# Sparse attention and a gated feed-forward block on one core: first loads, first mask, one pair's transposes and the written-out order are changed

## The chip, the core and the metric

The kernel runs on one core of a Trainium2 chip. The core has five engines with a queue of instructions each: TensorE (PE, matrix products and transposes), VectorE (DVE), ScalarE (ACT, here the exponentials, tanh and part of the copies), GpSimd (POOL, here masks at the start and the issue of the loads that convert fp32 to bf16) and SyncE (SP, which issues transfers and computes nothing). An engine takes its queue in order; an instruction that waits for a semaphore holds up everything behind it on that engine. The metric is the device time of the core in microseconds (us): the median of three runs. One more execution is recorded by the hardware profiler, and the profile, the trace and all durations come from that one.

## The reference

Inputs are q, k and v of 4 batches x 8 heads x 768 positions x 64, a table of three sampled blocks for each of 24 blocks of 32 positions, and the weights of the second half, in fp32.

```python
scores = scale * np.matmul(q, k.transpose(0, 1, 3, 2))
mask = np.abs(blk_i - blk_j) <= window
mask = mask | (blk_i == 0) | (blk_j == 0) | (blk_i == n_blocks - 1) | (blk_j == n_blocks - 1)
for qb in range(n_blocks):
    for kb in sampled_blocks[qb]:
        mask[qb * block:(qb + 1) * block, kb * block:(kb + 1) * block] = True
scores = np.where(mask, scores, -1000000000.0)
...
x = softmax(scores) @ v          # heads side by side: 4 x 768 x 512
h = np.maximum(x @ w_in, 0.0)    # 512 -> 1024
conv_out[s] = sum(conv_w[k] * h[s + k - 1] for k in range(3))
out = (h * sigmoid(conv_out)) @ w_out   # 1024 -> 512
```

## The kernel before

**Work and tiles.** Two heads of a batch make a pair; there are 16 pairs P0 to P15, four to a batch. Half a batch (384 query positions) is a segment; segment n has 18 units, the last half batch is split into a segment of 256 and one of 128 positions (12 and 6 units), 144 units in all. A unit is eight blocks of 128 x 128 scores: products on PE into a psum tile `st` (line 745, two operations `s`, six products in most units), one exponential of 128 x 1024 on ACT into `pt` (line 756, `exp`), and products with the values into `av` (line 778, two operations `av` of four products, the value tile carrying a column of ones for the sums). When all units of a pair in a segment are through, DVE takes the reciprocal and normalises into `xtok` (lines 695 and 697), and the result is transposed into `xT`: in segments 0, 7 and 8 on PE (line 716), in 1 to 6 by a transposing transfer that SP issues (line 706, called the x transfers here, four to a segment). Then come the products with w_in (line 886, `f1`, which needs all four transposed pieces of its segment), relu on ACT or DVE (lines 906 and 908), the convolution as three scaled copies and two additions on DVE (938, 946), tanh on ACT (985), the gate on DVE (988, 993), the products with w_out (824, `f2`; the last block 809), and the copy and transfer out (829 to 832).

**Mask.** A masked score gets -8000 added before the scaling, by 24 more rows of contraction: rows 64 to 87 of the query side hold a 24-row table of the allowed blocks, those of the key side the indicator of the block (`nblk`). The table `aadd` is made at the start: POOL writes the band and the last row (`A` and `row23`), DVE the edges (`a3`), and when the sampled blocks have landed, `a4` multiplies three comparisons with them into it (lines 294 to 300). Two groups of products (`w24`, line 314) spread it, and four copies (`m_q0`, `m_q1`, `m_k` twice) put the rows into the first slot tiles `e` and `o`; later slots copy them (`m_h1`, `m_slot`).

**Queries and keys.** Pairs below `NPE` (6 here) are transposed on PE: `kq_transposes` loads k and half of q, then 6 key transposes (line 472) and 4 query transposes (line 509) go through a psum tile, and DVE or ACT copies them into the slot (lines 342 and 346); the second query half is loaded later (`nq`) and takes 4 more transposes. The other pairs go through the crossbar: `kq_crossbar` loads k and q, two transposing transfers on SP (`xb`, line 584, first k, then q) write `stg`, and two copies of 64 x 1536 fill the slot. Pair 0's first loads are fp32 transfers on the hardware queues of SP and ACT (lines 253 to 261), cast by `cast_q` and `cast_k`; all other loads are issued by POOL and convert on the way. Some POOL loads have a small copy ahead of them (`pace`, lines 420 and 659) that holds the queue until an earlier load or an exponential is through.

**The order.** Nothing is scheduled at run time. The program builds a list of operations (1,796 of them, numbered as they are made), and the string ORDER says in which order they are put on the queues: two characters are the number of an operation to base 64, then a letter for the engine where it has a choice (P, A, V, G, S), then the buffer for each tile that it takes. `put_down` reads it. The order of the instructions on each engine is thus the order of the string. Ahead of the first products PE does `NWARM` products on zeros (line 1011).

Of the kernel before, what the change touches and what calls it, by code (L numbers as in the profile page):

```python
# [7 lines left out]
FP32 = mybir.dt.float32  # L8
# [3 lines left out]
ALU = mybir.AluOpType  # L12
# [8 lines left out]
0c00010d02030e0f0g1k01l1w01y10508090a0b06070H0I041z1K11M21N1Y21f01s10G0j0h0K0E0i0l0/V30qA11Arn1rorprqrrrsrtru  # L21
rvrwrxryrzrArBrCrDrErFrGrHrIrJrKrLrMrNrOrPrQrRrS13014A0rTrUrVrWrXrY0n00rA0pA12V19110V1aV0m01611bV15V0oArZr+r/
1c01dV0v0F0x0u17A18A1jV00ws0s1s2s34B04C4G11eA4D04H4L04M4I14N21m14E11p01nV11oV1qA1rV4Q14R4F4S34V04J4K4W4O52153
4P4T4U4X4570581A14Y5455900A0z0y1xV11BV21D05c15d4Z0555h05i561FV1CV1EV5e15j20s15q15r0t5s35a5b5f5g5v05w1O05k5A15B
5x41R15F05G0B4+01LV21PV35C51QV1TV1SV4/1g05l5K15L5H01hV1iV0k1t11vV1ZV31uV0V1+34i1/0W4j0X4k2a04l0Y4m1G04n0Z4o2c0
4p2d4q0+4r2o14s1U14t2q14u2r4v2w24w2y24x2z4y5m15n5M15t15T05u5U5V25y5z5005Y15Z0L15D5E5I610625J5N5O05W5+30C0M5P2
0U5Q661675X5o16346f06g51V06855pV0P5/606465696a6k16l6h06m16b06c0D5R06i16j6d16p06q5SA6u16v6r26w32bA46eVhJ1hK0J
hLV00OhM06z0hN0ThOVi506AhS16B4hT6H16IhUV6J5i6i76nhP06M0hQ6N1H1hRA6O0id1if1JV1IVi8i96o6R16s6ShV0hW6T16W06t6X721
hXA6Y2ia20121V4736xhY06y6ChZ6D06K7706L6P787430Q22Vie6E1igh+Vi216Q7c17d6U6V2306Zi36+7947e525A6Fih6/224Vil2706G1
i4A7h07i7m17517j0iih/11V0761WV1XV7ai07b7f7n7gi1A7o17u07v7k7l2e07w27z17A7p7q02h17B37E07F7J17K7G4imibit3iniu2fV0  # L30
ic0ij2gVioikip7r02jViv2iV7siw7L5iH07R07S7T0iqirixis7x7y7CiI7D7H7W17X7/080iB17IiC7M7N7U17Y1812712s02t7tiy7O17P
iz2pV0iA2xV10S2uV17Q2A12B7V841858907Z7+828aiJiD8638h18i8387888b48j58m08n8o02E04z2G2H32602J2I4AiEiK8c8r18s8w08x
iLA0iFV18e22vV8fiQ1iN0iOiR8t18y2iPAiSVj90jbja8E18F8d08k8J08KiW18liT08G38L48O18P8Q58p8q8u8T08U8V0iUiX2CV22DVjc
2FV2iVVjdiYA8Y18Z8v8z8A940j008H1iZ1j18+1jejh1jijjj2V8B0jk8C2O2k12R2P12S0959622U2T991i+8I8M9a8N2708R29V28Vjli/A
9b39e08S8W9f8X8/900979j19k9g49l5jm911jp2jfjqj61j79r0j8V92jsjr98j309s9c9d9h9w19x9i8g22K02V1938D2W2L9t09y12l1j4
2nV2mVj5Vjgjn9B09C9m9n9u19G19H9v9z9A9D29I39L09M9N5jt9o2jx3jyjoju9pjAjzjBjvjw9q9EjL19T19FjX09U9Y0jY9Z9J9V09+1jC
jM9K9O9P0a119Wa29Xa60a79/a0jNjZa33ae1a809Q1jDjEj+jOj/V2afaj0akk40a4a5k530311jPA3ag2k11k2a9ao1al3k3A12Z2+23332
383903b3c22MV32XV4k6V9R2YVkp02NVkqkrks0Napat0kj0auaq43e3dav5k71k8aaab0ackkk9AklAay1azaG0aHkm1knka0kbah1aiamaI1
aA0koVkcAktkN12QV3kx2kOkykAaL0aMkd1anaraskg0aN2kukzawkv2/V4aQ1aRaxaBaD2aS3aV0khkekiAkfAkF3kBaC0aJaKaOaWb11aX4
jR0b2jS9S0341iGb35kCjTaPb60jUb7aTjF1jVA1b81bb1aUaYbcaZjGkQkGkIkHaEbd2kw1kJkDa+1kEa/kPkRbg0bhbi3kKjHb41b5kV0b9  # L40
bl1bmbajIbt0jQiM353f03gjWaFadb0jJV3bn4kSbebfbjkWbuk/1by136V0kTkLkM3hV1kUbv5l0bkbzbobD03iV37Vbq2bEkXl1bA13j3m
3k13n03r3o3p3qbF0l23aV0l3A0bI1bJkYbQ0bRkZV1l81l9bK2bS3l50l6l7Abr3lV1laVlt0lulvlwlxbV1bWbp0le1bwb+0b/bxbBbX4c05
# [71 lines left out]
def kernel(  # L114
# [24 lines left out]
    SEQ = "nq0 nq1 k4 q4 w0 v4 w1 nq2 w2 k5 q5 w3 v5 nq3 k6 q6 v6 k7 q7 v7 nq4 nq5"  # L139

    CONV_PE = {8: (0, 1, 2, 3)}

    sb = ctx.enter_context(tc.tile_pool(name="sb", bufs=1))
# [903 lines left out]
```

## Time and profile before

| | |
|---|---|
| median of 3 runs | 213.57 us (213.3 to 215.49) |
| profiled execution | 214.17 us |
| its span, first to last instruction | 212.4 us |
| granted TensorE clock, mean | 0.999 |
| busy PE / DVE / ACT / POOL | 199.5 / 183.5 / 192.4 / 61.4 us |
| moved by DMA | 25.21 MB |

The page's second part shows the span in 40 slices of 5.3 us, busy share in tenths:

```profile
PE   8799999989999996999999997999999999999993
...
DVE  5889979999789985999999986999889939999870
ACT  5999999999999986999999996999999999997822
```

And its part on queues says which transfers there are: q0 holds POOL's converting loads, q1 the transfers of SP, q10 those of ACT.

```profile
q0 software_dynamic: 19728, 11.05, 43.4%
q1 hardware_dynamic: 30408, 13.05, 29.2%
q10 hardware_dynamic: 576, 0.69, 0.9%
```

In a row of the timeline stand start, length, engine, line, operation, output and inputs, shapes, count, and in brackets how long the engine stood idle before it and what released it. A busy PE is not PE at its peak, as its products overlap. Waits are inferred from semaphores.

### The profile page before, as it was taken

What the parts mean: (1) busy time and instruction counts of PE and PEld (TensorE: products, weight loads), DVE (VectorE), ACT (ScalarE), POOL (GpSimd) and SP (SyncE); (2) the same over time, 40 slices, a digit from 0 to 9 for tenths busy, and PEclk for the clock granted to TensorE, in tenths of its full rate; (3) what the DMA queues carried; (4) which work ended last, traced back from release to release, by engine and by line L of the source; (5) the groups of instructions that cost most, each with busy time, mean ns of one, the idle gap of its engine ahead of it and who ended that gap; (6) DMA issues with size and microseconds to landing.
All of it is one profiled execution on the core that took longest, in us unless ns stands there. A gap on an engine that the chain in (4) does not pass through costs nothing.

```text
span 212.4 us, 6868 instructions
## 1 busy us (share of the span) xinstructions
PE 199.5 (94%) x2708; PEld 155.6 (73%) x2727; DVE 183.5 (86%) x579; ACT 192.4 (91%) x253; POOL 61.4 (29%) x117
## 2 busy tenths in 40 slices
PE   8799999989999996999999997999999999999993
PEld 7689978877778774777688775777687877775752
DVE  5889979999789985999999986999889939999870
ACT  5999999999999986999999996999999999997822
POOL 8937456530732522300716363600000000000000
PEclk9999999999999999999999999999999999999999
DMA  6999999996899499894679999990231132020205
GB/s 169 184 197 200 165 115 116 124 146 95 112 141 119 90 138 117 154 202 106 90 99 173 124 133 210 209 176 20 65 93 22 22 128 91 0 84 28 94 0 198
DMA packets 50743, 25.21 MB, mean 119 GB/s; under 512 B 36800, under 2 KB 47768, under 8 KB 50712
## 3 DMA queue, kind: packets, MB, share of 16 engines
q0 software_dynamic: 19728, 11.05, 43.4%
q1 hardware_dynamic: 30408, 13.05, 29.2%
q10 hardware_dynamic: 576, 0.69, 0.9%
q8 instruction: 21, 0.34, 0.7%
q14 instruction: 10, 0.08, 0.1%
HBM read 23.08 MB, written 6.29 MB: 138 GB/s over the span
## 4 chain that ended last, share of the span: by engine, by line
PE 50%; DVE 20%; ACT 16%; DMA 9%; issue 4%; SPq 1%; ACTq 0%; DVEq 0%
PE st L745 15%; PE mix L824 11%; ACT pt L756 11%; PE mix L886 10%; PE av L778 8%; DMA xT<-xtok 6%; DVE m L938 5%; DVE m L946 3%; DMA stg<-nat 2%; DVE gT L993 2%; DVE hE L908 2%; DVE o L346 2%; PE st L1011 2%; ACT hE L906 1%; DVE e L346 1%
## 5 line engine op out<-in xcount | busy, mean ns | idle before, releaser
L756 ACT ACTIVATE pt<-st 128x1024 bf16<-128x1024 f32 x144 | 140.9, 1037 | 4.0 <-PE st L745 3.1
L778 PE MATMUL av<-vt,pt 128*128 128x65 bf16 x1152 | 61.8, 193 | 0.0
L778 PEld LDWEIGHTS <-pt 128*128 128x128 bf16 x1152 | 53.2, 97 | 11.4 <-issue 2.0
L886 PE MATMUL mix<-xT,winb 128*128 128x384 bf16 (+2 forms) x288 | 54.4, 307 | 4.0 <-DMA xT<-xtok 3.0
L938 DVE TENSOR_SCALAR m<-hE,cw 128x382 bf16<-128x382 bf16 (+2 forms) x192 | 50.1, 317 | 2.1 <-ACT hE L906 1.8
L745 PE MATMUL st<-o 88*128 88x128 bf16 (+1 forms) x240 | 44.8, 229 | 0.3 <-ACT pt L756 0.3
L824 PE MATMUL mix<-woutb,gT 128*128 128x512 bf16 x157 | 43.6, 379 | 1.3 <-DVE gT L993 0.3
L745 PE MATMUL st<-o,e 88*128 88x128 bf16 (+1 forms) x228 | 44.0, 233 | 0.3 <-ACT pt L756 0.2
L745 PE MATMUL st<-e,o 88*128 88x128 bf16 (+1 forms) x224 | 42.4, 234 | 1.2 <-ACT pt L756 1.2
L745 PE MATMUL st<-e 88*128 88x128 bf16 (+1 forms) x208 | 41.5, 239 | 0.5 <-ACT pt L756 0.2
L745 PEld LDWEIGHTS <-o 88*128 88x128 bf16 x464 | 34.7, 97 | 8.6 <-issue 1.7
L745 PEld LDWEIGHTS <-e 88*128 88x128 bf16 x436 | 33.8, 97 | 9.3 <-issue 0.9
L946 DVE TENSOR_TENSOR m<-m 128x764 bf16<-128x764 bf16 (+2 forms) x64 | 33.5, 532 | 0.3
L886 PEld LDWEIGHTS <-winb 128*128 128x128 bf16 x288 | 23.6, 97 | 10.0 <-issue 3.5
L985 ACT ACTIVATE m<-m 128x764 bf16<-128x764 bf16 (+2 forms) x32 | 26.4, 832 | 0.6 <-DVE m L946 0.6
L420 POOL COPY pace<-pt 1x1 bf16<-1x1 bf16 x24 | 8.3, 345 | 54.9 <-ACT pt L756 54.9
L824 PEld LDWEIGHTS <-gT 128*128 128x128 bf16 x184 | 15.3, 97 | 10.0 <-DVE gT L993 0.7
L906 ACT ACTIVATE hE<-mix 128x384 bf16<-128x384 f32 (+2 forms) x38 | 18.6, 503 | 3.9 <-PE mix L886 2.7
L908 DVE TENSOR_SCALAR hE<-mix 128x384 bf16<-128x384 f32 x26 | 14.2, 553 | 8.0 <-PE mix L886 7.0
L697 DVE TENSOR_TENSOR xtok<-av,rcp 128x384 bf16<-128x384 f32 (+2 forms) x36 | 18.2, 505 | 0.3
L993 DVE TENSOR_TENSOR gT<-m,hE 128x764 bf16<-128x764 bf16 (+3 forms) x36 | 18.0, 508 | 0.5 <-ACT hE L906 0.3
L240 POOL DMA_DIRECT2D nat<-in_q_dram x23 | 16.8, 733 | 3.3 <-issue 2.7
(93 smaller groups left out, 167.0 us busy)
## 6 DMA issues: line engine op xcount, KB each, us to landing
out_dram<-o2s SPq DMA_DIRECT2D x22, 256.0 KB, 2.1
nat<-in_k_dram POOLq DMA_DIRECT2D x15, 192.0 KB, 5.0
vn<-in_v_dram POOLq DMA_DIRECT2D x15, 192.0 KB, 5.5
nat<-in_q_dram POOLq DMA_DIRECT2D x6, 192.0 KB, 5.3
winb<-in_moe_w_in_dram POOLq DMA_DIRECT2D x2, 512.0 KB, 6.6
woutb<-in_moe_w_out_dram POOLq DMA_DIRECT2D x4, 256.0 KB, 4.9
nat<-in_q_dram POOLq DMA_DIRECT2D x9, 96.0 KB, 4.7
nq<-in_q_dram POOLq DMA_DIRECT2D x6, 96.0 KB, 4.6
```

Of the source, the lines that this page charges most:

```text
L697: nm = op("norm", {"DVE": t_dps(128 * C)}, lambda e: nc.vector.tensor_tensor(out=xtok_t[xk.index][:, 0:C].rearrange("p c h d -> p h c d"), ...
L745: nc.tensor.matmul(out=st[:, 128 * x:128 * (x + n_)], lhsT=QK[kc % 2][s][0:88, 1, hh, kc // 2, :], rhs=QK[par][s][0:88, 0, hh, idx:idx + n ...
L756: nc.scalar.activation(out=pt_t[ptb.index], in_=st_t[stb.index], func=AF.Exp, bias=0.0, scale=0.125)
L778: nc.tensor.matmul(out=o[:, off:off + 65], lhsT=pt_t[ptb.index][:, 128 * x:128 * x + 128], rhs=V_t[vslot_b[P].index][:, hh, kc, 0:65], sta ...
L824: nc.tensor.matmul(out=acc(), lhsT=gT_t[gb.index][:, ffc, 128 * t:128 * t + 128], rhs=woutb[:, ffc, :], start=(ffc == 0), stop=(ffc == NFF ...
L886: nc.tensor.matmul(out=mix_t[hb.index][:, w1 * y:w1 * y + w1], lhsT=winb[:, fc, 128 * ffc:128 * ffc + 128], rhs=xT_t[xt_buf[n].index][:, f ...
L906: nc.scalar.activation(out=dst, in_=src, func=AF.Relu, bias=0.0, scale=0.5)
L908: nc.vector.tensor_scalar(out=dst, in0=src, scalar1=0.5, scalar2=0.0, op0=ALU.mult, op1=ALU.max)
L938: nc.vector.tensor_scalar(out=m_t[cb.index][:, x, y, 0:w], in0=hE_t[heb.index][:, f0 + y, t0 + x:t0 + x + w], scalar1=cw[:, x, f0 + y:f0 + ...
L946: nc.vector.tensor_tensor(out=m[:, a_, :, 0:w], in0=m[:, a_, :, 0:w], in1=m[:, b_, :, 0:w], op=ALU.add)
L985: th = [op("tanh", {"ACT": t_act(2 * w) + 0.04}, lambda e, cb=cb, w=w: nc.scalar.activation(out=m_t[cb.index][:, 0, :, 0:w], in_=m_t[cb.in ...
L993: nc.vector.tensor_tensor(out=gT_t[gtb.index][:, f0:f0 + 2, t0:t1], in0=m_t[cb.index][:, 0, :, 0:w], in1=hE_t[heb.index][:, f0:f0 + 2, 1 + ...
```

## The change

Six things change.

1. **First loads.** The keys of head 1 (`k1`) move from ACT's queue to SP's, behind the sampled blocks; ACT issues only the first query load.
2. **First mask.** The table holds 1 for masked and 0 for allowed; -8000 is put into the key rows instead (`k_rows`). `a4` is one comparison of all three sampled blocks with the column index (24 x 3 x 24, integers) and one minimum over those three and `A`, in place of a cast and three multiplications; the cast of the column index (`col`, line 287) goes.
3. **One shorter transpose.** The second query transpose of pair 0, head 0 takes 64 columns instead of 128, so it no longer reads columns that belong to head 1's cast.
4. **Pair 5** goes through the crossbar (`NPE` 5): 6 key and 8 query transposes and their six copies are replaced by two transfers on SP and two staged copies; its second query half comes with the first load.
5. **Warm products**: 60 instead of 45.
6. **ORDER** is new throughout (1,803 operations).

```diff
-    NF, NPE = 4, 6
+    NF, NPE = 4, 5
...
-    NWARM = 45
+    NWARM = 60
...
     q0 = first_q(0, "ACT", -22, [])
-    k1 = first_k(1, "ACT", -21, [q0])
     ld_sb = op("ld_sb", {"SP": 0.46}, lambda e: nc.sync.dma_start(out=sbi, in_=sampled_blocks.bitcast(I32)), -21,
                after=[k0], lat=1.8)
-    q1 = first_q(1, "SP", -20, [ld_sb])
+    k1 = first_k(1, "SP", -20, [ld_sb])
+    q1 = first_q(1, "SP", -20, [k1])
...
     def a_rand(e):
-        nc.vector.tensor_copy(out=rf, in_=sbi[:, 0:6:2])
-        for r in range(3):
-            nc.vector.scalar_tensor_tensor(out=aadd if r == 2 else A, in0=colidx, scalar=rf[:, r:r + 1], in1=A,
-                                           op0=ALU.not_equal, op1=ALU.mult)
+        nc.vector.tensor_tensor(out=hit[:, 0:3], in0=colidx_i.unsqueeze(1).broadcast_to([NB, 3, NB]),
+                                in1=sbi[:, 0:6:2].unsqueeze(2).broadcast_to([NB, 3, NB]), op=ALU.not_equal)
+        nc.vector.tensor_reduce(out=aadd, in_=hit.rearrange("j r c -> j c r"), axis=mybir.AxisListType.X, op=ALU.min)
...
     def k_rows(dst, x):
-        return lambda e: dcopy(e, dst[64:88, 1, 0], nblk.rearrange("j (p c t) -> j t c p", c=3, t=2)[:, x])
+        def fn(e):
+            to, src = dst[64:88, 1, 0], nblk.rearrange("j (p c t) -> j t c p", c=3, t=2)[:, x]
+            if e == "ACT":
+                nc.scalar.activation(out=to, in_=src, func=AF.Copy, bias=0.0, scale=-8000.0)
+            else:
+                nc.vector.tensor_scalar(out=to, in0=src, scalar1=-8000.0, scalar2=None, op0=ALU.mult)
+        return fn
...
-                        nc.tensor.transpose(out=t[:, 128 * pos:128 * pos + 128], in_=src()[:, c0:c0 + 128], identity=ident)
+                        w_ = 64 if P == 0 and g == 0 and hh == 0 and y == 1 else 128
+                        nc.tensor.transpose(out=t[0:w_, 128 * pos:128 * pos + 128], in_=src()[:, c0:c0 + w_],
+                                            identity=ident)
```

ORDER can't be read by eye. Decoded by the numbering of the list, the old and the new string put these on the queues. On which engine operations stand that could stand on two:

| operation | before | after |
|---|---|---|
| copies of the mask rows (`m_k`, `m_q0`, `m_q1`) on ACT / DVE | 4 / 0 | 2 / 2 |
| half query casts of pair 0 on ACT / DVE | 0 / 2 | 1 / 1 |
| query copies on ACT / DVE | 3 / 23 | 6 / 16 |
| key copies on ACT / DVE | 3 / 11 | 3 / 9 |
| staged copies on DVE | 20 | 22 |
| value copies on ACT / DVE | 2 / 14 | 0 / 16 |
| relu on ACT / DVE | 38 / 26 | 37 / 27 |
| output copies on ACT / DVE | 16 / 9 | 18 / 7 |

PE's queue up to the first scores (k0, k1 key transposes of head 0 and 1, q likewise, a number for warm products), and ACT's:

```text
PE  before  32, k0, 6, w24, q0, w24, k1, 3, q1, 4, scores
PE  after   34, k0, 7, q0, w24, w24, 7, k1, 9, q1, 3, scores
ACT before  m_k, cast_k, k_cp, m_k, m_q1, m_q0, k_cp, k_cp, q_cp, exp, exp, exp, q_cp, exp ...
ACT after   cast_k, m_k, k_cp, q_cp, q_cp, cast_q, m_q1, k_cp, k_cp, q_cp, q_cp, exp, exp, exp, exp ...
```

SP's queue (x2.3 is the fourth x transfer of segment 2, P9q the query transfer of pair 9; transfers out and small ones left out):

```text
before  x1.0 x1.1 P6k P6q x1.2 x1.3 P7k P7q x2.0 P8k P9k x2.2 x2.1 P9q P8q x2.3 x3.0 P10k P10q P11k P11q
        x3.2 x3.1 x3.3 P12k P12q x4.0 P13k x4.1 P13q x4.2 x4.3 x5.0 P14k P14q P15k x5.1 P15q x5.2 x5.3 ...
after   x1.0 P5k P5q x1.1 P6k P6q x1.2 x1.3 P7k P7q x2.0 P8k P8q P9k x2.1 x2.2 x2.3 P9q x3.0 P10k P10q x3.1 P11k
        x3.2 P11q x3.3 x4.0 P12k P12q P13k x4.2 x4.1 x4.3 P13q P14k P14q x5.0 x5.1 P15k P15q x5.2 x5.3 ...
```

And what PE has in its queue between a segment's last value product and its first `f1` (half units of scores, `av` and `f2` operations; segment 2 has one more `f1` step after):

| segment | before | after |
|---|---|---|
| 2 | 16 s, 14 av, 8 f2 | 16 s, 13 av, 8 f2 |
| 3 | 14 s, 9 av, 11 f2 | 12 s, 9 av, 9 f2 |
| 4 | 14 s, 15 av, 8 f2 | 14 s, 13 av, 6 f2 |
| 5 | 9 s, 10 av, 10 f2 | 10 s, 3 av, 7 f2 |
| 6 | 12 s, 9 av, 6 f2 | 11 s, 7 av, 7 f2 |

On POOL the loads begin, before, k1 q1 v1 k2 q2 v2 k3 q3 v3 nq0 nq1, half of w_in, k4, then the first pace copy; after, k1 q1 v1 k2 nq0 q2 nq1 v2 k4, the first pace copy (which waits for nq0), k3 q3 q4 v3 and both halves of w_in.

More of the change, by code (lines that the diff above doesn't have):

```diff
@@ L26 @@
[L26 to L40, printed above, removed]
@@ L62 @@
+qM0qlA1qrA3qsqmqSqNqJqZ0qOqTq+q/r31r0r1A0r2Sr4r5r6r7A2r8Sr90rarbrcrdAreA
 """
```

84 lines of the change are left out of this document (48 added, 36 removed).

## The prediction

> **What bounds the kernel now.** I read the page first, then the busy time of stretches, the chain of waits, the waits in total, and the timeline of the head, engine by engine.
>
> ```profile
> 7.74:20.00 12.26, 10.77 (x183) 9.77 (x183) 10.92 (x25) 12.21 (x14) 7.12 (x13) 1.00 1.34 196
> 40.00:60.00 20.00, 19.41 (x286) 15.69 (x286) 17.75 (x54) 19.91 (x25) 7.08 (x14) 1.00 1.01 125
> 80.00:100.00 20.00, 18.09 (x234) 13.33 (x234) 17.90 (x55) 18.17 (x25) 2.88 (x5) 1.00 0.86 145
> 120.00:140.00 20.00, 18.55 (x252) 14.27 (x251) 17.30 (x51) 17.79 (x22) 9.14 (x17) 1.00 1.18 180
> 140.00:160.00 20.00, 19.89 (x248) 14.53 (x250) 18.13 (x55) 19.52 (x26) 0.00 (x0) 1.00 0.37 72
> ```
>
> Each row gives the stretch, its length, then busy time of PE, weight loads, DVE, ACT and POOL, the granted clock and the DMA traffic. From 7.74 to 20 ACT is full (12.21 of 12.26) and PE is not (10.77). From 40 to 60 PE and ACT are both 97% busy or more, so what relieves only one of them buys little. From 80 to 100 and from 120 to 140 both lose time together: 1.9 and 1.5 us of PE, 1.8 and 2.2 of ACT. The chain of waits (start, length, what) and the list of waits say for what:
>
> ```profile
> 74.93 7.55 DMA xT<-xtok
> ...
> 123.55 6.01 DMA xT<-xtok
> ```
> ```profile
> PE mix L886 <- DMA xT<-xtok: 3.0, 2, 1.7
> ```
>
> Two transposing transfers of normalised attention (xT<-xtok) hold the chain for 7.55 and 6.01 us, and PE's products with w_in (L886) stand 3.0 us for them, in two waits of which the longer is 1.7 and so the other 1.3. They belong to segments 2 and 4 (half a batch each, counted from 0). They are the largest holes between the first exponential, at 7.74, and the tail. The head before 7.74 is a chain of its own. ACT, PE's weight loads and DVE there:
>
> ```profile
> 2.96 0.70 ACT L342 COPY e<-nblk 24x384 bf16<-24x384 bf16 x1
> 3.69 0.51 ACT L342 CAST nat<-o2s 128x384 bf16<-128x384 f32 x1
> 4.63 0.47 ACT L342 COPY e<-mix 64x384 bf16<-64x384 bf16 x1 [0.43 <-PE mix L472]
> ```
> ```profile
> 0.99 3.18 PEld L1011 LDWEIGHTS <-warm 128*128 128x128 bf16 x32 [0.99 <-DVE warm L222]
> 4.25 0.17 PEld L472 LDWEIGHTS <-nat 128*128 128x128 bf16 x3
> 4.38 0.38 PEld L1011 LDWEIGHTS <-warm 128*128 128x128 bf16 x6
> ```
> ```profile
> 6.52 0.52 PEld L745 LDWEIGHTS <-e 88*128 88x128 bf16 x7
> ```
> ```profile
> 3.81 0.16 DVE L295 CAST rf<-sbi 24x3 f32<-24x3 int32 x1 [1.11 <-DMA sbi<-in_sampled_blocks_dram]
> 4.00 0.50 DVE L297 SCALAR_TENSOR_TENSOR A<-colidx,rf,A 24x24 f32<-24x24 f32 x2
> 4.53 0.23 DVE L297 SCALAR_TENSOR_TENSOR aadd<-colidx,rf,A 24x24 bf16<-24x24 f32 x1
> ```
> ```profile
> 5.53 0.26 DVE L346 CAST nat<-o2s 128x192 bf16<-128x192 f32 x1 [0.33 <-PE mix L509]
> ```
>
> ACT has work from 2.96 on and waits only once, 0.43 us for the first key transposes; the first score's weights are loaded from 6.52, over a microsecond before the exponential.
>
> **The change, part by part. The head: mask, first loads, warm products.** The mask took DVE from 3.81 to 4.76. In its place come a comparison over 24x72 and a minimum over 24x96, which no row shows; the 24x24 steps took 0.23 each and the operands are three and four times as long, so I take 0.5 for the two, with 0.4 and 0.95 (no gain) as ends. DVE gets 0.45 us, and the 0.33 at 5.53 goes, since the shortened transpose no longer reads the columns that this cast overwrites. Head 1's keys are loaded from SP behind the block indices, about 0.5 us later; in DVE's new order they are cast after the mask and a query cast, which covers that. The first key cast no longer stands behind the copy at 2.96, so it can start up to 0.7 us sooner.
>
> PE takes this back. Its queue now has 34 warm products before the first transpose (32 before) and 26 between that and the first score (13 before). The later ones take 0.38 / 6 = 0.063 us, so first transpose 4.25 + 2 x 0.063 = 4.38, and the stretch to the first score, 6.52 - 4.25 = 2.27, grows by 13 x 0.063 = 0.82 and loses at most the 0.33 that stood behind DVE: first score 7.1 instead of 6.5. The first exponential came 1.22 us after the first score's weights, of which the first unit takes the 0.52 of that row and some 0.2 to drain; so PE allows it at 7.8. On ACT two copies leave the stretch behind 4.63 (the other 0.70 mask copy and one of the mask rows), and three short query copies and half a cast come, which is about even: 4.8 + (7.74 - 4.63) = 7.9, less the waits that go. **Head: 0**, ends -0.4 and +0.5.
>
> Rows and a rule meet here: 32 products took 3.18 us (0.099 each), those from 4.38 on 0.063, so the array sped up at about 4.3. The Trainium skill, "TensorE: Matmul & The Clock Gate", Part 1, says that the warm-up is a budget of about 3.4 us of time and not a number of matmuls. By that rule 15 more products buy no clock and only lengthen PE's queue; where ACT doesn't cover them, the sum would be 0.4 us worse.
>
> **Work taken off the engines.** Pair 5 goes from TensorE's transposes to the crossbar. 6 + 8 transposes leave PE, at 0.17 / 3 = 0.057 each 0.8 us.
>
> ```profile
> L346 DVE COPY e<-mix x16: 276/409/551, 5.7 to 70.2; 64x256 bf16<-64x256 bf16 x7, 64x768 bf16<-64x768 bf16 x5, 64x512 bf16<-64x512 bf16 x4
> L346 DVE COPY vt<-vn x13: 320/353/552, 13.1 to 148.6; 128x768 bf16<-128x768 bf16 x13
> L346 DVE COPY e<-stg x10: 542/548/564, 53.1 to 149.3; 64x1536 bf16<-64x1536 bf16 x10
> ```
> ```profile
> L906 ACT ACTIVATE hE<-mix 128x384 bf16<-128x384 f32 x30 | 14.6, 504 | 2.7 <-PE mix L886 2.3
> ...
> L342 ACT COPY o2s<-mix 128x512 f32<-128x512 f32 x13 | 7.6, 595 | 0.9 <-PE mix L824 0.8
> ...
> L342 ACT COPY vt<-vn 128x768 bf16<-128x768 bf16 x2 | 1.7, 852 | 0.0
> ```
>
> By the first of these rows (0.55 the longest form, 0.41 the middle, 0.28 the shortest) DVE drops 2 x 0.55 + 2 x 0.41 + 2 x 0.28 = 2.5 us of copies for the pair and takes two staged ones, 1.1: it gains 1.4, and two value copies of 0.35 take half of that again. The new order moves those (2 x 0.85) and one relu (0.50) from ACT to DVE, two output copies (2 x 0.595) the other way: ACT loses 1.0. As all three busy engines lose work, none stands in the way of PE's **-0.8**; ends -1.0 and 0. Pair 5's two transfers stand on SP between segment 1's first and second x transfer; SP spends about 1.3 us on each (two in 2.56, row below), so the second goes out up to 2.5 us later. Two more of the segment follow, which end the wait for it: 0. Pair 5's loads keep their places, with its second query half in one load now.
>
> **Early exponentials.**
>
> ```profile
> 10.59 0.45 ACT e L342
> ```
>
> This query copy, between the third exponential and the fourth in the chain, goes to DVE: **-0.45**, as PE has 1.5 us of holes from 7.74 to 20 and DVE 1.3; 0 at the other end, if PE's order takes over. On POOL the first pace copy now stands ahead of pair 3's loads. It waits for pair 0's second query half, which is POOL's fifth load instead of its tenth, so it should pass several microseconds sooner: 0, and 1 us if pair 3's keys come after their transposes.
>
> **The x transfers.** This term decides.
>
> ```profile
> 72.32 2.56 SPq L584 DMA_TRANSPOSE stg<-nat  x2
> ```
> ```profile
> 120.47 1.64 SPq L584 DMA_TRANSPOSE stg<-nat  x1
> ```
> ```profile
> DMA to landing us min/median/max: 2.3/5.0/6.6
> ```
> ```profile
> 91.23 0.65 PE mix L886 x4
> 91.89 0.48 PE av L778 x16
> 92.37 0.44 PE st L745 x6
> 93.47 0.86 PE mix L824 x4
> ```
>
> Both late transfers were issued close behind transfers of pairs (9 and 8 at 72.32, 13 at 120.47); the third row holds the landings of all x transfers. In the new order pair 9's query and pair 13's come behind the last x transfer of segments 2 and 4. I let those land in the median, 5.0, with 2.3 and 7.55 as ends. Against that stands the cover: PE's work in its queue between a segment's last value product and its first L886, priced by the last four rows (0.44 a unit of scores, 0.03 a value product, 0.16 and 0.215 a product of L886 and L824): segment 2 8.7 us before and 8.9 after; 3 8.9 and 7.6; 4 8.4 and 7.3; 5 7.5 and 5.6; 6 6.3 and 6.3. Before, segment 2 needed 8.7 + 1.7 = 10.4, its 7.55 and 2.8 more; segment 4 8.4 + 1.3 = 9.7, its 6.01 and 3.7 more. So I count 3 us beside the landing. After: segment 2 needs 8 of 8.9, and its 1.7 go. Segment 4 needs 8 of 7.3: of 1.3, 0.8 stay. Segment 3's last x transfer now stands right behind pair 11's query: at 5.0 to 6.0 it needs 8 to 9 of 7.6, and I take 0.6. Segment 5 falls where POOL issues nothing (its column is 0 from 140 to 160) and where 2.3 is the better guess: 5.3 of 5.6; I take 0.2. Sum -1.7 - 0.5 + 0.6 + 0.2 = **-1.4**, ends -3.0 and +5.
>
> **Tail.** From the last twelve units on, PE's list holds the same operations in another order: 0, ends -0.7 and +0.7.
>
> Sum: 0 - 0.8 - 0.45 - 1.4 = -2.6 us. The profiled execution took 214.17 (its span of 212.4 and 1.8 around it), so 211.5 for it; the median, 213.57, lies 0.6 lower: **211.0**.
>
> **The rivals.** *The x transfers land late and the new order covers them less (slower).* If they land in 6.6, and in 7.55 behind a pair's, segment 3 stalls 3 + 7.55 - 7.6 = 2.9, segment 4 3 + 6.6 - 7.3 = 2.3, segment 2 0.7, segment 5 at the median 2.4: 8.3 instead of 3.0, +5.3 less 1.25 of saved work, 217.6. It decides from a landing of 4.6 on in segment 3 and 2.6 in segment 5. For it: three covers shrink. Against: both old culprits move behind. 0.20.
>
> *Only work goes.* The stalls wander but keep their 3 us: -0.8 to -1.25, 212.5. For it: PE and ACT at 97% and more from 40 to 60 leave an order little to find. 0.18.
>
> *The warm products set the head*, by the rule above, worked out from rows: 15 x 0.063 = 0.9 on PE's queue, of which 0.4 to 0.9 come through, 211.4 to 211.9. 0.06.
>
> *More goes:* both stalls without new ones, the head 0.4 and the tail 0.7 sooner: -0.8 - 0.45 - 3.0 - 1.1 = -5.3, 208.2. 0.12.
>
> **How the numbers follow.** The forecast keeps 0.44, between 209.6 and 211.8. A measurement here tells about 1% from no change, 211.4 and 215.7. Of the 0.44 I put 0.36 below 211.4; with 0.12 from the last rival, faster has 0.48. Within 1%: 0.08 + 0.18 + 0.06, and 0.03 of the first rival at a small size, 0.35. Slower 0.17. The range reaches from 208.4, by the last rival, to 215.6, short of most of the first.
>
> **What would show it.** First exponential within 0.4 us of 7.74, with the first score's weights near 7.1; 14 transposes fewer at L472 and L509; no copy between the third exponential and the fourth; the wait of L886 for xT<-xtok down from 3.0 to about 1.6, none of it in segment 2. I am wrong if that wait grew, in segments 3 and 5 above all, if the first score came past 7.5, or if ACT and PE both stayed as full and the span moved by less than 1 us.

## The result and the profile after

| | before | changed |
|---|---|---|
| median | 213.94 us (4 runs) | 210.92 us (4 runs) |
| ratio, 95% interval | 1 | 0.9897 (0.9855 to 0.9940) |
| profiled execution | 214.17 us | 210.87 us |
| its span | 212.4 us | 209.0 us |

The changed kernel is about 1% faster, and 0.1 us from the forecast. Disturbed executions are left out of all ratios here; one profile below, of the kernel before once more, comes from such an execution, and single rows of it are read, not its time. First the page's part 4 of the kernel before, the shares of the chain that ended last, by engine:

```profile
PE 50%; DVE 20%; ACT 16%; DMA 9%; issue 4%; SPq 1%; ACTq 0%; DVEq 0%
```

Then the page of the changed kernel: busy time, PE's slices, and the same part 4.

```profile
PE 199.7 (96%) x2709; PEld 156.5 (75%) x2728; DVE 184.0 (88%) x571; ACT 191.9 (92%) x254; POOL 62.0 (30%) x115
...
PE   8998999889999999999999999999999999999993
...
PE 73%; DVE 17%; ACT 7%; issue 2%; ACTq 0%; DVEq 0%
```

No transfer is left on the chain: DMA had 9% of it and has none. The holes of PE in the middle are gone; two slices between 37 and 47 us are at 8 now. The stretches that the prediction showed, now of the changed kernel:

```profile
7.74:20.00 12.26, 11.04 (x186) 9.80 (x183) 11.35 (x26) 11.59 (x15) 8.52 (x15) 1.00 1.22 165
40.00:60.00 20.00, 18.49 (x279) 14.83 (x280) 18.80 (x55) 19.37 (x24) 9.40 (x15) 1.00 1.10 140
80.00:100.00 20.00, 19.83 (x260) 14.97 (x261) 19.23 (x58) 19.58 (x27) 3.87 (x8) 1.00 0.81 134
120.00:140.00 20.00, 19.89 (x254) 14.84 (x254) 19.11 (x56) 19.11 (x25) 8.45 (x16) 1.00 1.18 157
```

From 80 to 100 PE went from 18.09 to 19.83 and from 120 to 140 from 18.55 to 19.89, the two stretches with the late x transfers. From 40 to 60 it went the other way, 19.41 to 18.49.

As stretches at fixed times hold different work in the two kernels, I split both at three events: the first exponential, the 25th and the last (the 144th). The kernel before, then the changed one:

```profile
7.74:32.40 24.66, 23.17 (x375) 20.24 (x375) 21.70 (x66) 24.42 (x28) 14.19 (x27) 1.00 1.19 171
...
32.40:193.51 161.11, 155.04 (x2128) 119.91 (x2145) 145.47 (x435) 153.13 (x194) 40.33 (x75) 1.00 0.73 112
...
193.51:212.40 18.89, 14.66 (x134) 9.63 (x134) 11.58 (x46) 9.29 (x22) 0.00 (x0) 0.99 0.23 84
```
```profile
9.07:34.42 25.35, 23.43 (x378) 20.11 (x376) 20.80 (x61) 23.82 (x27) 12.94 (x24) 1.00 1.13 161
...
34.42:191.91 157.49, 154.59 (x2125) 120.11 (x2141) 148.03 (x444) 152.56 (x196) 41.79 (x74) 1.00 0.76 114
191.91:209.00 17.09, 13.64 (x126) 8.72 (x125) 9.40 (x39) 9.82 (x22) 0.00 (x0) 0.98 0.34 124
```

The second column is the length, and its differences are the whole result:

| stretch | forecast | profile | difference before to after |
|---|---|---|---|
| start to first exponential | 0 | +1.33 | 7.74 to 9.07 |
| first to 25th exponential | -0.45 | +0.69 | 24.66 to 25.35 |
| 25th to last exponential | -0.8 - 1.4 = -2.2 | -3.62 | 161.11 to 157.49 |
| last exponential to the end | 0 | -1.80 | 18.89 to 17.09 |
| sum | -2.65 | -3.40 | 212.4 to 209.0 |

So the total came out by luck, by errors of opposite sign: the front lost 2.0 us where 0.45 was to be won, and the middle and the tail won 3.2 more than forecast. By the third column, PE's busy time, the middle won nearly all of its 3.62 us out of PE's idle time, which fell from 6.07 to 2.90 us; the busy time fell by 0.45. (The pair's -0.8 is put in the middle whole; part of it would lie in the early stretch.)

The head of the changed kernel, by PE's weight loads, ACT and DVE (start, length, ..., in brackets the idle time ahead):

```profile
4.81 0.79 PEld L1016 LDWEIGHTS <-warm 128*128 128x128 bf16 x7
...
6.89 0.39 PEld L1016 LDWEIGHTS <-warm 128*128 128x128 bf16 x7 [0.20 <-issue]
...
8.20 0.49 PEld L750 LDWEIGHTS <-e 88*128 88x128 bf16 x7
```
```profile
3.55 0.51 ACT L345 CAST nat<-o2s 128x384 bf16<-128x384 f32 x1 [1.08 <-DMA o2s<-in_k_dram]
4.09 0.72 ACT L335 ACTIVATE e<-nblk 24x384 bf16<-24x384 bf16 x1
5.16 0.47 ACT L345 COPY e<-mix 64x384 bf16<-64x384 bf16 x1 [0.36 <-PE mix L475]
6.26 0.36 ACT L345 COPY e<-mix 64x256 bf16<-64x256 bf16 x1 [0.63 <-PE mix L513]
...
9.07 4.84 ACT L761 ACTIVATE pt<-st 128x1024 bf16<-128x1024 f32 x5
```
```profile
3.69 0.22 DVE L293 TENSOR_TENSOR hit<-colidx_i,sbi 24x72 f32<-24x72 int32 x1 [0.72 <-DMA sbi<-in_sampled_blocks_dram]
3.94 0.31 DVE L295 TENSOR_REDUCE aadd<-hit 24x24 bf16<-24x96 f32 x1
```

The mask's two steps take 0.22 and 0.31. Seven warm products take 0.79 from 4.81 on (0.113 each) and 0.39 from 6.89 on (0.056): in this execution the array sped up in between. In the profile of before it did so near 4 us (the prediction read 4.3 off the rows; the trace records the full clock from 3.95 on). The first score's weights are loaded at 8.20, past the 7.5 that was named as a sign of error. ACT waits 1.08 us for the keys, then does the mask copy of 0.72 that it did ahead of them before.

### The profile page after: what moved, and what is told of

It reads as the page before. It is cut to its first block, busy times and chain, and to the rows that moved or that the text cites. A ratio compares the mean times of both kernels' runs of the same rounds, so it can differ in the third digit from the quotient of the medians.

```text
span 209.0 us, 6855 instructions
## 1 busy us (share of the span) xinstructions
PE 199.7 (96%) x2709; PEld 156.5 (75%) x2728; DVE 184.0 (88%) x571; ACT 191.9 (92%) x254; POOL 62.0 (30%) x115
## 3 DMA queue, kind: packets, MB, share of 16 engines
q0 software_dynamic: 19712, 11.05, 44.5%
## 4 chain that ended last, share of the span: by engine, by line
PE 73%; DVE 17%; ACT 7%; issue 2%; ACTq 0%; DVEq 0%
PE st L750 22%; PE mix L829 17%; PE mix L891 15%; PE av L783 12%; DVE m L943 5%; ACT pt L761 5%; DVE m L951 2%; DVE e L349 2%; PE st L1016 2%; DVE hE L913 2%; DVE o L349 2%; DVE xtok L702 1%; PE mix L814 1%; PE st L829 1%; PE mix L513 1%
## 5 line engine op out<-in xcount | busy, mean ns | idle before, releaser
L783 PE MATMUL av<-vt,pt 128*128 128x65 bf16 x1152 | 60.9, 193 | 0.2
L891 PE MATMUL mix<-xT,winb 128*128 128x384 bf16 (+2 forms) x288 | 54.1, 308 | 0.4 <-DVE hE L913 0.3
L943 DVE TENSOR_SCALAR m<-hE,cw 128x382 bf16<-128x382 bf16 (+2 forms) x192 | 50.3, 322 | 0.4
L829 PE MATMUL mix<-woutb,gT 128*128 128x512 bf16 x157 | 44.7, 379 | 0.9
L750 PE MATMUL st<-o,e 88*128 88x128 bf16 (+1 forms) x228 | 43.0, 233 | 1.2 <-DVE o L349 0.9
L891 PEld LDWEIGHTS <-winb 128*128 128x128 bf16 x288 | 23.4, 97 | 7.4 <-issue 0.8
L423 POOL COPY pace<-pt 1x1 bf16<-1x1 bf16 x24 | 6.8, 285 | 47.2 <-ACT pt L761 47.1
L911 ACT ACTIVATE hE<-mix 128x384 bf16<-128x384 f32 (+2 forms) x37 | 18.0, 503 | 1.3 <-PE mix L891 0.7
L913 DVE TENSOR_SCALAR hE<-mix 128x384 bf16<-128x384 f32 x27 | 14.9, 554 | 3.1 <-PE mix L891 1.8
```

Of the source, the lines that this page charges most:

```text
L750: nc.tensor.matmul(out=st[:, 128 * x:128 * (x + n_)], lhsT=QK[kc % 2][s][0:88, 1, hh, kc // 2, :], rhs=QK[par][s][0:88, 0, hh, idx:idx + n ...
L783: nc.tensor.matmul(out=o[:, off:off + 65], lhsT=pt_t[ptb.index][:, 128 * x:128 * x + 128], rhs=V_t[vslot_b[P].index][:, hh, kc, 0:65], sta ...
L829: nc.tensor.matmul(out=acc(), lhsT=gT_t[gb.index][:, ffc, 128 * t:128 * t + 128], rhs=woutb[:, ffc, :], start=(ffc == 0), stop=(ffc == NFF ...
L891: nc.tensor.matmul(out=mix_t[hb.index][:, w1 * y:w1 * y + w1], lhsT=winb[:, fc, 128 * ffc:128 * ffc + 128], rhs=xT_t[xt_buf[n].index][:, f ...
L911: nc.scalar.activation(out=dst, in_=src, func=AF.Relu, bias=0.0, scale=0.5)
L913: nc.vector.tensor_scalar(out=dst, in0=src, scalar1=0.5, scalar2=0.0, op0=ALU.mult, op1=ALU.max)
```

## The experiments

Each ran against the kernel before on the same chip; ratios are those, with their 95% interval. Order edits are shown as the queue that they change.

### The changed kernel again

No edit.

> The changed kernel once more, for its head. In the two profiled executions the products at the start were spaced 0.1 us apart until 4 us (before) and until 6.9 us (changed); the first exponential came at 7.74 and 9.07. Theory: the moment at which the array speeds up is drawn anew in each execution, so here the first exponential comes anywhere from 7.6 to 9.2 us. Rival: the changed head itself makes it late, then 9.07 within 0.1 again. Both: 0.985 to 0.993 of the time before.

Measured: 210.26 us, ratio 0.9865 (0.9818 to 0.9912). The profiled execution, 212.19 us with a span of 210.3, was the longest of the six. First exponential 8.99, tail 17.08, no wait for an x transfer, but in the place of it one of DVE for pair 5's staged keys:

```profile
50.68 0.55 DVE L349 COPY e<-stg 64x1536 bf16<-64x1536 bf16 x1 [1.75 <-DMA stg<-nat]
```

The short tail and, in part at least, the head's lateness are thus properties of the kernel, and the wait for staged keys shows a place in segment 1 that is only just covered.

### Is it SP's neighbour? Two orders of SP alone

The prediction put the late x transfers down to the pair transfers issued just ahead of them. In the changed kernel two of these were put back in front:

```diff
 SP   ... x2.1 x2.2
-x2.3 P9q
+P9q x2.3
 ... x4.1
-x4.3 P13q
+P13q x4.3
```

> The changed kernel with two swaps on SP's queue alone: pair 9's query transfer ahead of segment 2's last x transfer, pair 13's ahead of segment 4's, as in the kernel before. Theory (these neighbours made the landings late): PE's wait of L891 for xT<-xtok comes back with 1 to 3 us and the time rises by 0.8 to 2.5 us, to 0.994 to 1.0 of before. Rival (the place on SP does not matter, the order of the work does): no wait over 0.3 us, 0.985 to 0.992.

Measured: 211.60 us, ratio 0.9914 (0.9880 to 0.9948). No wait of PE for an x transfer at all, so the theory of the forecast failed here; DVE waits 2.4 us for pair 5's staged keys, as in the copy above. The median lies 1.3 us above the copy's on the same chip, with intervals that overlap; what that comes from is open. And in the kernel before the pair transfers were put behind:

```diff
 SP   ... x2.2 x2.1
-P9q P8q x2.3
+x2.3 P9q P8q
 ... x4.1
-P13q x4.2 x4.3
+x4.2 x4.3 P13q
```

> The kernel before with the opposite swaps on SP alone: pair 9's and pair 8's query transfers behind segment 2's last x transfer, pair 13's behind segment 4's. Theory: the wait of L886 for xT<-xtok falls from 3.0 to under 1.0 us, and the time by 1 to 2.5 us, to 0.988 to 0.995. Rival: the wait stays at 2 us and more, or it goes and another takes its place; 0.997 to 1.003.

Measured: 219.98 us, ratio 1.0318 (1.0270 to 1.0366). SP's rows show segment 2's last x transfer, now ahead of the two pair transfers:

```profile
75.82 1.18 SPq L706 DMA_TRANSPOSE xT<-xtok  x1
77.09 2.58 SPq L584 DMA_TRANSPOSE stg<-nat  x2
```

The wait for x transfers is gone here too, and three others grew. The list of waits (total, times, longest):

```profile
DVE e L346 <- DMA stg<-nat: 8.6, 3, 4.8
ACT pt L756 <- PE st L745: 6.5, 9, 3.9
PE mix L886 <- DVE hE L908: 6.0, 3, 3.6
```

The staged keys and queries now land late; DVE stands 4.8 us for one of them, the relu behind it on DVE's queue comes late, and PE stands 3.6 us for that. So moving the pair transfers does clear the x transfers, but hands the wait to the other stream, and PE stands 6.0 us for that relu instead of 3.0 for x transfers. (A stretch at half the clock comes on top; see the last section.) And the neighbour alone doesn't make an x transfer late: with pair 9's and pair 13's query back in front in the changed kernel, none was. Something beside it must have been there before.

### POOL's order alone

Four loads issued by POOL lie around segment 2's last x transfer (issued at 74.93) in the kernel before. POOL's rows there, of the kernel before:

```profile
72.55 0.70 POOL L240 DMA_DIRECT2D nat<-in_k_dram  x1
...
73.37 0.71 POOL L240 DMA_DIRECT2D vn<-in_v_dram  x1
...
74.23 0.76 POOL L240 DMA_DIRECT2D nat<-in_q_dram  x1
...
76.89 0.70 POOL L240 DMA_DIRECT2D vn<-in_v_dram  x1 [0.33 <-DVE m L988]
```

The edit takes the kernel before and gives POOL's queue alone the changed sequence from pair 8's query load on; all other queues keep theirs.

```diff
 POOL, from 72 to 82 us
-k v q v
+k q
```

> The kernel before with POOL's queue alone put in the changed kernel's sequence from pair 8's query load on (each other engine keeps its sequence). In the profile before POOL issued four loads between 72.5 and 77.6 us, around segment 2's last x transfer, and in the changed kernel two, the values of the one pair sooner and of the other later. Theory (the burst of loads made that transfer land late): the wait of L886 for xT<-xtok falls from 3.0 to under 1.5 us, none of it in segment 2, and the time by 1 to 2.5 us, 0.988 to 0.996. Rival (loads are not it, the work on the other engines came too late for the order): wait 2 us or more, 0.997 to 1.004.

Measured: 212.47 us, ratio 0.9944 (0.9905 to 0.9982). POOL's rows and the wait:

```profile
73.36 0.72 POOL L240 DMA_DIRECT2D nat<-in_k_dram  x1
...
75.04 0.76 POOL L240 DMA_DIRECT2D nat<-in_q_dram  x1
```
```profile
PE mix L886 <- DMA xT<-xtok: 0.7, 2, 0.5
```

The wait fell from 3.0 to 0.7, none of it in segment 2. With SP's and PE's queues as before, and the pair transfers still in front, thinning the loads was enough to clear segment 2. The reverse was tried too: the changed kernel with POOL in the sequence of before.

```diff
 POOL, from 72 to 82 us
-k q
+k v q v
```

> The changed kernel with POOL's queue alone put back in the sequence of the kernel before from there on. Theory: PE waits again for xT<-xtok, 1 to 3 us, and the time rises to 0.992 to 1.0 of before. Rival: no such wait over 0.3 us, 0.983 to 0.991.

Measured: 211.26 us, ratio 0.9921 (0.9874 to 0.9969). No wait came back in segment 2 (0.4 us did in segment 1), so this expectation of my theory failed: POOL issued four loads from 73.97 to 79.23, segment 2's last x transfer went out among them, and it landed in 4.7 us. Its row on SP, and the last line of the view of its tile:

```profile
76.35 1.18 SPq L711 DMA_TRANSPOSE xT<-xtok  x1
```
```profile
DMA to landing us min/median/max: 4.7/4.7/4.7
```

So neither alone is enough. Put together, the profiles fill a table for segment 2's last x transfer, with the time from its issue to the last landing record that the trace has of it, in us:

| | four loads around it | two loads around it |
|---|---|---|
| pair transfers just ahead of it | before: 7.55, and 7.38 in its second profile (below); PE waits 1.7 and 1.9 | before with POOL's new sequence 4.9, changed with pair 9's query (one transfer) in front 5.0; no wait |
| pair transfers behind it | before with these behind 5.5, changed with POOL's old sequence 4.7; no wait | changed 4.5, and 4.1 to 5.0 over the eight profiles with its order there; no wait |

It was late only with both, the pair transfers directly ahead and the four loads beside; in the kernel before, taking away either clears it. Putting both back into the changed kernel was not tried. For segment 4's last x transfer the picture is alike but not as clean: 6.0 and 6.2 us before, 4.4 with the pair's transfer behind, 4.3 with POOL's new sequence; yet in the changed kernel with pair 13's query in front and four loads around, it landed in 3.9, so a count of loads doesn't say it all. In the times, POOL's sequence alone is worth 0.6%, and without it the changed kernel keeps 0.8 of its 1.0 to 1.4%; the intervals overlap, so whether the parts add up can't be told from these runs.

### The tail

The changed kernel up to the 132nd exponential, then the remaining 275 operations in the sequence of before.

```diff
-ORDER from the 132nd exponential on: new
+ORDER from the 132nd exponential on: that of before
```

> The changed kernel up to the 132nd exponential, then the 275 operations that are left in the sequence that they have in the kernel before (buffers given anew). From the last exponential to the end the profiles show 18.9 us before and 17.1 changed. Theory: the new sequence of the tail is worth these 1.8 us, so 0.995 to 1.0 of before. Rival: the tail is set by PE's sum of work, and what it gained comes from what was done ahead of it: 0.986 to 0.992.

Measured: 212.28 us, ratio 0.9936 (0.9901 to 0.9971), and 2.0 us above the copy of the changed kernel on the same chip. From the last exponential to the end it took 18.4 us, against 17.1 in all nine profiles that have the new tail and 18.6 to 18.9 in the four of before. ACT's copy of the last w_out products of segment 7 shows where the time goes, first of this run, then of the changed kernel:

```profile
205.52 0.59 ACT L345 COPY o2s<-st 128x512 f32<-128x512 f32 x1 [2.99 <-PE st L829]
```
```profile
204.31 0.58 ACT L345 COPY o2s<-st 128x512 f32<-128x512 f32 x1 [1.26 <-PE st L829]
```

The new tail is worth 1.3 us in the profiles and 0.7% in the times; the term that I had put at 0 with ends of 0.7 was too small. It isn't order alone: with the old tail, two copies of w_out products stand on DVE again (1.29 us for the two) that the changed kernel has on ACT. The two weren't taken apart, and 0.5 us of the tail's 1.8 came with what lies ahead of it.

### The transposes that were saved

Pair 4's 14 transposes are done twice, so that PE has as many as before.

```diff
-                        nc.tensor.transpose(...)
+                        for _ in range(2 if P == 4 else 1):
+                            nc.tensor.transpose(...)
```

> The changed kernel with pair 4's 6 key and 8 query transposes done twice, so PE has the 14 back that left it with pair 5. Theory: PE sets the time in these stretches, +0.8 us against the changed kernel, 0.989 to 0.994 of before. Rival (PE waits for others there anyway): no change, 0.985 to 0.989.

Measured: 211.37 us, ratio 0.9927 (0.9889 to 0.9965); span 208.2. The profiled execution, 210.09 us, is the shortest of the twelve. The ratio lies where the theory expected it, 1.1 us in the medians above the copy of the changed kernel; but that ran on another chip, and the intervals overlap. The profile doesn't settle it either. In all other runs of this order PE waited 0.35 to 0.9 us for a DVE copy near 44.5; here that wait is gone, and in its place stand 0.39 us of wait for ACT and four of the extra transposes. It stays open whether the 0.8 us come through.

### The warm products

44 instead of 60 warm products, placed nearly as before.

```diff
-PE  34, k0, 7, q0, w24, w24, 7, k1, 9, q1, 3, scores
+PE  32, k0, 6, q0, w24, w24,    k1, 3, q1, 3, scores
```

> The changed kernel with 44 products on zeros instead of 60: 32 ahead of the first transpose and 12 between that and the first score, 7 and 7 and 9 before. Theory (the extra products are only time in PE's queue, 0.1 us each while the array is slow): first exponential 0.6 to 1.6 us earlier than in the changed kernel when the array speeds up at the same moment, and 0.4 to 1.2 us of it at the end, 0.981 to 0.986 of before. Rival (they are needed for the speed): the array speeds up later or not before the scores, time as the changed kernel or longer, 0.986 to 0.995.

Measured: 210.38 us, ratio 0.9880 (0.9826 to 0.9933), the same as the changed kernel within the interval. The first exponential came at 8.62, with a speed-up as early as 3.65; so the extra products aren't what holds it there. ACT's rows suggest what is:

```profile
4.29 0.73 ACT L335 ACTIVATE e<-nblk 24x384 bf16<-24x384 bf16 x1
5.04 0.74 ACT L345 COPY e<-mix 64x384 bf16<-64x384 bf16 x2
...
6.35 0.35 ACT L345 CAST nat<-o2s 128x192 bf16<-128x192 f32 x1 [0.29 <-DMA o2s<-in_q_dram]
```

The key copy starts at 5.04, right behind the mask copy (before: 4.63, behind a wait), and head 1's query cast waits for a load that now stands fourth on SP's queue instead of third.

### The query copy, the mask, and the kernel before once more

Three runs on one chip. One query copy of pair 1 back on ACT between the third and the fourth exponential:

```diff
-ACT  exp exp exp exp       DVE  ... q_cp ...
+ACT  exp exp exp q_cp exp  DVE  ...
```

> The changed kernel with one early query copy put back on ScalarE, between the third exponential and the fourth, where the kernel before had it; VectorE gives it up. By the forecast's step (0.45 us of ScalarE's time there come through to the end, since ScalarE sets the early stretch): +0.45 us against the changed kernel, and first to thirteenth exponential 0.3 to 0.5 us longer. By the rival, that VectorE's chain of slot copies sets the early stretch once ScalarE is relieved: 0, or up to 0.4 us less, with ScalarE's idle time near 18 us smaller.

Measured: 210.37 us, ratio 0.9863 (0.9816 to 0.9909): no difference. The twelve exponentials up to the 13th took 12.26 us with the copy on ACT, and 12.44 and 12.54 in the two profiles of the changed kernel. The rival was right: the copy's 0.45 us on ACT cost nothing up to there. Up to the 25th this profile took 25.95, the most of the ten with this order (25.2 to 25.95), so a term of this size can't be read from one profile. The same profile also shows segment 1 again, this time with a wait for an x transfer:

```profile
59.25 0.32 PE L891 MATMUL mix<-xT,winb 128*128 128x384 bf16 x1 [1.25 <-DMA xT<-xtok]
```

The old mask arithmetic in the changed kernel:

```diff
-tensor_tensor(hit[:, 0:3], colidx_i, sbi, not_equal)
-tensor_reduce(aadd, hit, min)
+tensor_copy(hit[:, 0], colidx_i); tensor_copy(rf, sbi)
+for r in range(3): scalar_tensor_tensor(aadd if r == 2 else A, hit[:, 0], rf[:, r], A, not_equal, min)
```

> The changed kernel with the mask's sampled blocks worked in as before: column index copied to fp32 ahead, sampled blocks copied to fp32, three steps of 24x24, in place of the comparison of 24x72 and the minimum over 24x96. VectorE then takes about 0.9 us for it instead of 0.53. By the forecast (the 0.4 us saved on VectorE are covered, as ScalarE and TensorE's queue set the first score): first exponential within 0.2 us of the changed kernel's at a like moment of the array's speed-up, time the same within 0.3 us. By the rival (VectorE's mask is on the path to the first score): first exponential 0.4 us later and the time up by as much.

Measured: 210.68 us, ratio 0.9896 (0.9853 to 0.9939); the steps from the landing to the table took 0.95 instead of 0.56, and the first exponential came at 8.45, no later than in the other runs of this head. As forecast, the mask's saving is covered.

The kernel before, no edit:

> The kernel before once more, for one look at its head. If the array's speed-up falls at a moment of its own in each execution, the warm products shorten at another moment than in the first profile (there near 4.0 us), and the first exponential moves with it by up to half of that. If the moment belongs to the kernel, both come within 0.1 us of the first profile's, 7.74 for the exponential.

Its weight loads of the warm products and its first exponentials:

```profile
0.99 3.33 PEld L1011 LDWEIGHTS <-warm 128*128 128x128 bf16 x32 [0.99 <-DVE warm L222]
...
4.59 0.55 PEld L1011 LDWEIGHTS <-warm 128*128 128x128 bf16 x6
...
8.06 1.94 ACT L756 ACTIVATE pt<-st 128x1024 bf16<-128x1024 f32 x2
```

The six products behind the first transposes took 0.092 each, against 0.063 in the first profile: the speed-up came later, and the first exponential with it, 8.06 instead of 7.74. It took 217.1 us; its x transfers are in the table above, and its clock is looked at in the last section. The trace also records the granted clock; its first record of the full clock stands at 3.95 us in the first profile and at 4.95 here. (The stretches' clock column shows 1.00 even ahead of that record, so the spacing of the products is the thing to read.) All profiles, as first record of the full clock and first exponential:

| head | record / first exponential, us |
|---|---|
| of before | 3.95 / 7.74, 4.80 / 8.05, 4.95 / 8.06, 5.49 / 8.14 |
| changed | 4.03 / 8.31, 4.11 / 8.88, 4.13 / 8.65, 4.82 / 8.80, 5.86 / 8.99, 6.01 / 9.04, 6.86 / 9.07 |
| changed, old mask | 4.39 / 8.45 |
| changed, 44 warm products | 3.65 / 8.62 |

At like moments the changed head is 0.6 to 1.1 us later; from early to late moments either head loses some 0.4 us. The profile of before had the earliest moment of its kind and that of the changed kernel the latest, so its +1.33 is some 0.8 of the kernel and the rest of the draw.

### A mended head

From the kernel with 44 warm products, the mask copy goes back into the wait for the keys, and head 1's queries ahead of its keys.

```diff
-ACT  cast_k m_k k_cp ...
+ACT  m_k cast_k k_cp ...
-SP   k0 sampled_blocks k1 q1 v
+SP   k0 sampled_blocks q1 k1 v
```

> The kernel with 44 warm products, with two operations of the head moved: ScalarE copies the first mask rows of the keys (0.72 us) ahead of the first key cast, in the time in which it waits for the keys' landing anyway, as in the kernel before, and SyncE issues head 1's query load ahead of head 1's keys. Theory (what makes the changed head late is that this copy now stands between the key cast and the key copy, 0.4 us, and that the query cast waits for a load that is fourth on SyncE's queue, 0.3 to 0.4 us): first exponential 0.4 to 0.7 us sooner than the 8.62 us of the kernel with 44 warm products, no wait of ScalarE for the query load above 0.1 us, time lower by as much. Rival (VectorE's chain of casts and copies sets the first score, 0.1 us behind): first exponential not before 8.5 us, ScalarE waits for TensorE's transposes instead, time the same.

Measured: 210.87 us, ratio 0.9866 (0.9829 to 0.9903), not different from the kernel with 44. Its first exponential came at 8.96, and the run doesn't decide: the array was at half rate through the whole head (three warm products took 0.36 us from 7.43 on, 0.12 each; first record of the full clock at 10.07).

```profile
2.48 0.72 ACT L335 ACTIVATE e<-nblk 24x384 bf16<-24x384 bf16 x1
...
4.95 0.47 ACT L345 COPY e<-mix 64x384 bf16<-64x384 bf16 x1 [0.84 <-PE mix L475]
...
6.48 0.35 ACT L345 CAST nat<-o2s 128x192 bf16<-128x192 f32 x1
```

The copy does lie in the wait for the keys now and the query cast waits for nothing, but the slow transposes take up what was gained. By its numbers the run looks like the rival of the expectation: first exponential past 8.5, a wait of ACT for the transposes, the time the same. Whether 0.4 us come through with an early speed-up stays open. No version was measurably faster than the changed kernel.

## Why the prediction was right, point by point

**The total was right by luck: the head, the early exponentials and the tail were wrong, the work off the engines wasn't shown, and the x transfers had the right sign for half of the reason.**

**Head: 0 forecast, some 0.8 of the kernel's own and 1.33 in the profile.** The step that failed is "the first key cast no longer stands behind the copy at 2.96, so it can start up to 0.7 us sooner". The cast starts when the keys land, at 3.55 to 3.75 in the changed head, and started at 3.69 before. The copy had lain in the wait for them and cost nothing; now it stands behind the cast and in front of the key copy. In the run with the pair transfers in front, which had an early speed-up (4.03) and no wait of ACT, ACT was busy without a break from 3.67 on, and the key copy came at 4.95 instead of 4.63 and the first exponential 3.36 us after it instead of 3.11: its list, taken as "about even", is a quarter of a microsecond longer. The query load, one place later on SP, wasn't priced at all. That ACT's longer list is the cause is read from the rows; the run that should have shown it, the mended head, didn't decide. PE's side held where the speed-up was early: in that run the first score's weights came at 7.16, forecast 7.1, and ACT was later. Where the speed-up is late, products priced at 0.063 take 0.113.

The rule of the Trainium skill that was weighed, "TensorE: Matmul & The Clock Gate", Part 1 (time and not number of matmuls warms the array), isn't contradicted: 16 products fewer gave the same time (0.9880 against 0.9865 and 0.9897). The rival built on it, that the extra products set the head, isn't borne out, as without them the first exponential came no sooner (8.62, with the earliest speed-up of all); ACT's list bounds the head as much.

**Work off the engines: -0.8 forecast, not shown.** The 14 transposes are gone (36 to 30 and 48 to 40 weight loads at the two lines). PE's busy time from the 25th exponential to the last fell by 0.45 us. Doubling 14 others gave 0.9927, but the intervals overlap, and its profile shows no clear loss.

**Early exponentials: -0.45 forecast, +0.69 in the profile** (25.2 to 25.95 us in the ten profiles of the new order, 24.7 to 25.1 in the four of the old). The copy between the third and the fourth exponential is gone as said (five run from 9.07 without a break), and putting it back didn't make the run longer. My other end, "0, if PE's order takes over", was nearer: ACT now waits for scores.

```profile
18.39 2.92 ACT L761 ACTIVATE pt<-st 128x1024 bf16<-128x1024 f32 x3 [0.61 <-PE st L750]
```

Why the stretch became longer than before, and not only no shorter, was not tested.

**x transfers: -1.4 forecast, -3.0 in the profile; the sign was right and the reason half of it.** The wait of L891 for xT<-xtok is gone altogether, not down to 1.6, and segments 3, 4 and 5, where I counted 0.6, 0.8 and 0.2, have none. The step that failed is the one that made 5.0 us of landing out of "both late transfers were issued close behind transfers of pairs": that is half of the condition. The row that I read (72.32, two pair transfers) had four loads of POOL beside it, and the prediction didn't count them. The covers were priced well: from the last value product of segments 2 to 5 to their first L891 the changed kernel takes 9.3, 7.5, 7.1 and 5.5 us, for 8.9, 7.6, 7.3 and 5.6. The landings were not: the last x transfers land in 4.5, 3.8, 3.4 and 2.4 us, where I had 5.0, 5.0 to 6.0, 5.0 and 2.3. The 3 us that I counted beside each landing fit the middle two alone; from the last value product to the issue it takes 5.1, 2.5, 3.2 and 1.3 us. So segment 2, at 9.6 us in all, is only just covered: the landing, at 81.32, falls into its first group of L891 (from 81.06).

**Pair 5 on SP: 0 forecast.** In the changed kernel's own profile this holds, but of ten profiles with this order in segment 1, two show 1.4 and 1.5 us of wait for its x transfers and two 1.8 and 2.4 us for staged keys. From the 37th exponential to the 67th these four took 37.2 to 37.8 us, the others 35.4 to 36.0. So part of the gain is lost there in some executions. For the x transfers the traces point at POOL once more: in both (old mask, query copy on ACT) a pace copy let three loads go together between 50.3 and 52.4, and the third x transfer, issued at 51.6 and 51.75 among them, landed in 7.3 and 7.45 us. With POOL's old sequence three loads fell there too and it landed in 6.2; in the other seven profiles, with two loads at most within 3 us of its issue, it landed in 2.3 to 4.7. No run changed that alone, and why the staged keys come late stays open.

**Tail: 0 forecast, -1.8 in the profile.** "The same operations in another order: 0" was the error; the new tail, with two copies moved to ACT, is worth 1.3 of it by the run with the old one.

**The rivals.** That the x transfers land late and are covered less in segments 3 to 5 didn't come about; the cover was thin in segment 1, which it had left out, and in segment 2. "Only work goes" falls with the wait. "More goes" (208.2) had both stalls and the tail right and the head wrong.

## What to carry to other kernels

When a transfer lands late, look at every queue that issues transfers in that stretch, not only at its neighbour on its own: here two causes were needed; thinning the loads won 0.6%, and moving the transfers of the kernel before lost 3.2%, as another stream came late in their place. A copy that lies in a wait for a landing is free, and can cost time as soon as it stands behind that landing (here the next copy came 0.3 us later for a copy of 0.72). An order that leaves a transfer just covered is right in one profile and late in the next, so read several before a term below 1% is believed.

## What the hardware showed beside

**The moment of the speed-up is drawn anew in each execution.** With PE busy from 1.0 us on in every run, the full clock was first recorded between 3.65 and 6.86 us, and at 10.07 in one with 44 warm products. The Trainium skill, "TensorE: Matmul & The Clock Gate", Part 1, has the window running freely, which the runs agree with, and a spread of 0.5 us around 4 us of activity, which is too narrow for them (2.7 to 5.9 us from the first product on, and once 9.1).

**A short stall can halve the clock.** In the kernel before once more, PE stood 1.90 us for segment 2's x transfer; two stretches of it (length, busy PE, ..., then the granted clock as third column from the end):

```profile
80.00:83.00 3.00, 1.55 (x21) 1.16 (x20) 0.45 (x1) 2.43 (x3) 0.83 (x2) 1.00 1.80 153
83.00:87.00 4.00, 3.55 (x20) 2.31 (x20) 3.64 (x9) 1.12 (x2) 0.06 (x1) 0.57 0.59 89
```

The trace records half the clock from 83.46 for 3.41 us. In the run with the pair transfers behind, where PE stood 3.64 us, the same came from 87.41 on, again for 3.41 us. The first profile of before, with a wait of 1.7, shows none, and neither does a second stall of the very execution above, 1.94 us up to 132.51. So a stall of about 2 us can cost more than its length, but need not; what decides isn't shown. The same part of that page warns of PE-idle gaps beyond some 3.4 us; here the half clock followed a gap of 1.90, in one execution.
